# Ten x buffers, and a new order of openings, row copies and weight decode at the start of a convolution-gate kernel

## The chip, the cores and the metric

The kernel runs on one core of a Trainium2 chip. A core has five engines that run side by side, each taking its own instructions in order: TensorE (PE, matrix products; PEld in the profile is its weight load), VectorE (DVE), ScalarE (ACT), GpSimd (POOL) and SyncE (SP, which here only issues transfers). Sixteen DMA engines move data between the main memory and the core's memory SBUF, and inside SBUF. Matrix products are written to PSUM, which has eight banks. The metric is the time of one execution on the device in microseconds (us), smaller is better.

## What is computed

The input x has 8 sequences of 4224 positions with 192 channels. Two stages follow each other:

```python
# stage 1: a causal 7-tap convolution, taps by softmax, one set for each of 8 heads of 24 channels
w = exp(weight - weight.max(-1)); w = w / (w.sum(-1) + 1e-9)
x = einsum('hk,bskhg->bshg', w, windows_of_7(x))
# stage 2: a gated projection
gate = sigmoid(sum_k conv_w[k] * x[s - 4 + k])       # causal, 5 taps, each channel by itself
out = (gate * (x @ w_val)) @ w_out                   # two 192 x 192 products
```

All of it is float32.

## The kernel before

**Layout.** The sequences are joined into two long streams of 4 sequences each, which are computed side by side. 192 channels don't fit on 128 partitions, so 128 channels of both streams stand in a tile `x1` (two parts of columns), and the other 64 channels of both streams stand in `x2` (64 partitions for each stream).

**Superblocks and blocks.** The streams are cut into 13 superblocks (`NJS` has their sizes: 2, 3, ten times 5, 2), and each superblock into blocks of at most 502 columns: 2 blocks for each of superblocks 0 and 1, 3 for superblocks 2 to 11, one for the last. That makes 35 blocks. Block 0 and 1 have 304 and 302 columns, 2 and 3 have 448, the others 502, the last 364.

**Convolution (stage 1).** For each superblock the input comes as tiles `x_i` (`load_x`, line 131): four for superblock 0, then eight for each, one head apiece; they live in a pool of `XBUFS` buffers. `conv_unit` (line 271) computes a unit: four products of a window of x with a band matrix of the taps into one PSUM tile `pc` (line 285; each product stands as two instructions in the profile), and one copy on ACT from PSUM into `e` (line 294). Superblock 0 has 4 units, superblock 1 has 6, the others 10. As soon as a head is complete, `scatter` (line 306) issues the row copies: transfers from `e` to the rows of `x1` and `x2` (line 318, `x<-e` in the profile), on SP, or for heads 5 to 7 of the first three superblocks on POOL. Next to it `load_x` fetches the tile that takes the freed buffer.

**Gate and products (stage 2).** For each block n:
- `gate_open(n, i)` (line 343): ACT multiplies the x columns by the first of the five taps into a PSUM tile, `pa` (i = 0, both parts of `x1`) or `pb` (i = 1, `x2`). There is one `pa` and one `pb`. It needs the row copies of the block's superblock.
- `gate_taps` (line 354): DVE adds the other four taps (line 359).
- `gate_close` (line 364): ACT takes the sigmoid into `g1` or `g2` (line 372).
- `split` (line 458): ACT rounds x to its high part (lines 380, 388), POOL subtracts to get the low part (lines 381, 389), so that three fast products stand for one exact product.
- `diagonal`, `main`, `columns`, `rows` (lines 408 to 456): PE's products with `w_val` (what = "v") and `w_out` (what = "o"), into three PSUM tiles for each block and weight.
- `gated(n, q)` (line 464): DVE multiplies gate and value (line 468), which frees the PSUM tile of the value. `split_gated1` and `split_gated2` split the result.
- `project(n, q)` (line 478): ACT copies the output out of PSUM (line 484) and SP stores it.

The PSUM tiles of units, values and outputs share one pool of five buffers (`ps`, line 113).

**Weights.** They arrive as 64-bit floats, as pairs of integers. `decode` (line 203) makes float32 of them with nine DVE instructions (lines 212 to 222) on 128 x 384 elements and five more (line 228); `cast` (line 253) rounds the high part on ACT (line 255) and subtracts on DVE (line 256).

**Order.** The order of every engine's instructions is the order in which they are written; nothing is rearranged. The prologue (lines 514 to 532) decodes the small weights and `wv`, convolves superblocks 0 and 1, decodes `wo`, and opens the gates of blocks 0 and 1. Then step n of the main loop (line 534) works on the value of block n, the output of block n-1, the taps of block n+1, the opening of block n+2, and convolves `todo` units of the superblock that comes two after the one in work (`due`, line 505): 5 units in each of steps 0 to 3, then 3 or 4.

Of the kernel before, what the change touches and what calls it, by code (L numbers as in the profile page):

```python
# [81 lines left out]
PERM += [5 * HC + i for i in range(8, HC)]  # L82
QUADS = ((6, 7, 5, 0), (1, 2, 3, 4))
PER_LOAD = {2: 2, 3: 1, 5: 1}
XBUFS, EBUFS = 6, 3
LAG = 2
BY_POOL = 3

# [2 lines left out]
def kernel(  # L91
# [39 lines left out]
    def load_x(upto):  # L131
        while loaded[0] < min(upto, len(loads)):
            i = loaded[0]
            loaded[0] += 1
            g, hs, o = loads[i]
            f = len(hs) * NJS[g] * M
            t = xtiles[i] = xin.tile([WK, NMAX * M], F32, tag="x", name=f"x_{i}")
            nc.sync.dma_start(t[:, :f], xw[o : o + WK * f].rearrange("(p f) -> p f", f=f))
# [23 lines left out]
    def load_raw(name):  # L162
        nc.sync.dma_start(raw[name][1], raw[name][2])

    load_raw("cw")
    load_raw("wv")
    load_x(4)
    load_raw("wo")
    load_x(XBUFS)

    one = cp.tile([128, 1], F32, name="one")
# [86 lines left out]
    w_val, w_out = Weight("wv"), Weight("wo")  # L258
# [10 lines left out]
    first_unit = [next(i for i, u in enumerate(units) if u[0] == g) for g in range(NG)] + [len(units)]  # L269

    def conv_unit(u):
        g, q, ws = units[u]
        n = NJS[g]
        if u == first_unit[g]:
            x1s[g] = xp.tile([128, 2 * XB], F32, tag="x1", name=f"x1_{g}")
            x2s[g] = xp.tile([128, XC], F32, tag="x2", name=f"x2_{g}")
        if ws[0] == (0, 0):
            es[g, q] = ep.tile([M, 4 * NMAX * WIN], F32, tag="e", name=f"e_{g}_{q}")
        e = es[g, q]
        pc = ps.tile([128, 512], F32, tag="p", name=f"pc_{u}")  # L280
        for k, (hi, j) in enumerate(ws):
            h = QUADS[q][hi]
            i, at = home[g, h]
            c = (at * n + j) * M
            nc.tensor.matmul(  # L285
                pc[:M, k * WIN : (k + 1) * WIN],
                lhsT=xtiles[i][:, c : c + M],
                rhs=band[:, 4 * q + hi, :],
                start=True,
                stop=True,  # L290
            )
        a = (ws[0][0] * n + ws[0][1]) * WIN
        w = len(ws) * WIN
        nc.scalar.copy(e[:, a : a + w], pc[:M, :w])  # L294
        done = [hi for hi, j in ws if j == n - 1]
        for hi in done:
            h = QUADS[q][hi]
            i, at = home[g, h]
            last = at == len(loads[i][1]) - 1
            if last and g >= BY_POOL:  # L300
                load_x(i + 1 + XBUFS)
            scatter(g, h, e[:, hi * n * WIN : (hi + 1) * n * WIN])
            if last and g < BY_POOL:
                load_x(i + 1 + XBUFS)
# [28 lines left out]
    def views(n, k=KG - 1):  # L333
        g, o, m = STEPS[n]
        b = second(NJS[g])
        x1v = x1s[g][:, : 2 * b].rearrange("p (a t) -> p a t", a=2)
        return x1v[:, :, o + k : o + k + m], x2s[g][:, o + k : o + k + m]
# [5 lines left out]
    def gate_open(n, i):  # L343
        if n >= N:
            return
        m = STEPS[n][2]
        if i == 0:
            acc = ps_g.tile([128, 2, 512], F32, tag="pa", name=f"pa_{n}")[:, :, :m]
        else:
            acc = ps_h.tile([128, 512], F32, tag="pb", name=f"pb_{n}")[:, :m]  # L350
        accs[n, i] = acc
        nc.scalar.mul(acc, views(n, 0)[i], cwt[:, i, 0:1])  # L352

    def gate_taps(n, i, k0=1, k1=KG):
        if n >= N:
            return
        acc = accs[n, i]
        for k in range(k0, k1):
            nc.vector.scalar_tensor_tensor(  # L359
                out=acc, in0=views(n, k)[i], scalar=cwt[:, i, k : k + 1],  # L360
                in1=acc, op0=ALU.mult, op1=ALU.add,
            )

    def gate_close(n, i):
        if n >= N:
            return
        m = STEPS[n][2]
        if i == 0:
            dst = g1s[n] = gp.tile([128, 2, MB], F32, tag="g1", name=f"g1_{n}")[:, :, :m]
        else:  # L370
            dst = g2s[n] = gp.tile([128, MB], F32, tag="g2", name=f"g2_{n}")[:, :m]
        nc.scalar.activation(dst, accs.pop((n, i)), AF.Sigmoid)  # L372
# [35 lines left out]
    def diagonal(what, n):  # L408
        if not ok(n):
            return  # L410
        acc = bank(what, n, 2)
        w, _, _, h2, l2 = operands(what, n)
        r = slice(W22, W22 + 128)
        for i, (a, b) in enumerate(parts(w, h2, l2)):
            nc.tensor.matmul(acc, lhsT=a[:, r], rhs=b, start=(i == 0), stop=False)  # L415

    def main(what, n, q):
        if not ok(n):
            return
        fresh = (what, n, q) not in banks  # L420
        acc = bank(what, n, q) if fresh else banks[what, n, q]
        w, h, l, _, _ = operands(what, n)
        r = slice(W11, W11 + 128)
        for i, (a, b) in enumerate(parts(w, h, l)):
            nc.tensor.matmul(  # L425
                acc, lhsT=a[:, r], rhs=b[:, q], start=(fresh and i == 0), stop=(not fresh and i == 2)
            )
# [14 lines left out]
    def columns(what, n):  # L442
        if not ok(n):
            return
        m = STEPS[n][2]
        acc = banks[what, n, 2]
        w = w_val if what == "v" else w_out
        x = views(n)[0] if what == "v" else g1s[n]
        cuts = [m * i // 4 for i in range(5)]
        for i in range(4):  # L450
            c = slice(cuts[i], cuts[i + 1])
            for q, p in enumerate(HALVES):
                nc.tensor.matmul(  # L453
                    acc[p, c], lhsT=w.f[:, W12 : W12 + 64], rhs=x[:, q, c],
                    start=False, stop=(i == 3),
                )

    def split(n):
        if n >= N:
            return  # L460
        x1, x2 = views(n)
        xs[n, 1], xs[n, 2] = split1(sp, "x", n, x1), split2(sp, "x", n, x2)

    def gated(n, q):
        if not ok(n):
            return
        v = g1s[n][:, q] if q < 2 else g2s[n]
        nc.vector.tensor_tensor(out=v, in0=banks.pop(("v", n, q)), in1=v, op=ALU.mult)  # L468

    def split_gated1(n):  # L470
        if ok(n):
            pr[n, 1] = split1(pp, "p", n, g1s[n])

    def split_gated2(n):
        if ok(n):
            pr[n, 2] = split2(pp, "p", n, g2s[n])

    def project(n, q):
        if not ok(n):
            return  # L480
        m = STEPS[n][2]
        if n not in ots:
            ots[n] = op.tile([128, 3 * MB], F32, tag="ot", name=f"ot_{n}")
        nc.scalar.copy(ots[n][:, q * m : (q + 1) * m], banks.pop(("o", n, q)))  # L484
        o = 3 * sum(s[2] for s in STEPS[:n])
        if n == LAST:
            nc.sync.dma_start(out[:, o + q * m : o + (q + 1) * m], ots[n][:, q * m : (q + 1) * m])
        elif q == 1:
            nc.sync.dma_start(out[:, o : o + 3 * m], ots[n][:, : 3 * m])
# [3 lines left out]
    first = [next(n for n in range(N) if STEPS[n][0] == g) for g in range(NG)] + [N]  # L493
# [3 lines left out]
    done = [0]  # L497

    def conv(k):
        for _ in range(k):  # L500
            if done[0] < len(units):
                conv_unit(done[0])
                done[0] += 1
# [11 lines left out]
    put(cwt.rearrange("p a k -> p (a k)"), pr_cw, 0, 128, 0, 2 * KG)  # L515
    w_val.decode()
    conv(first_unit[1])
    w_val.cast()
    conv(2)
    w_out.decode()  # L520
    conv(1)
    gate_open(0, 0)
    gate_open(0, 1)
    gate_taps(0, 0)
    gate_taps(0, 1)
    split(0)
    w_out.cast()
    conv(first_unit[LAG] - done[0])
    gate_close(0, 0)
    gate_close(0, 1)  # L530
    gate_open(1, 0)
    gate_open(1, 1)

    for n in range(N + 1):
        todo = max(0, (due[n] if n < N else 0) - done[0])
        diagonal("v", n)
        gate_taps(n + 1, 0, 1, 3)
        split(n + 1)
        diagonal("o", n - 1)
        main("v", n, 0)  # L540
        main("v", n, 1)
        gate_taps(n + 1, 0, 3, KG)
        columns("v", n)
        gated(n, 2)
        gate_close(n + 1, 0)
        gate_open(n + 2, 0)
        columns("o", n - 1)
        split_gated2(n)
        project(n - 1, 2)
        rows("v", n)  # L550
        gated(n, 0)
        gated(n, 1)
        rows("o", n - 1)
        split_gated1(n)
        main("o", n - 1, 0)
        gate_taps(n + 1, 1)
        project(n - 1, 0)
        main("o", n - 1, 1)
        project(n - 1, 1)
        conv(todo)  # L560
        gate_close(n + 1, 1)
        gate_open(n + 2, 1)


# [88 lines left out]
```

## Time and profile before

| | us |
|---|---|
| median of 3 runs | 406.97 (405.59 to 406.98) |
| the profiled execution | 406.11 |
| its span in the profile | 404.3 |
| PE busy | 373.3 (92% of the span) |
| DVE busy | 347.1 (86%) |
| ACT busy | 320.3 (79%) |
| POOL busy | 249.7 (62%) |
| mean granted clock of PE | 0.974 of full speed |
| moved by DMA | 82.49 MB, 204 GB/s |

How to read the rows of the profile. A row of the order of instructions has the start and the length in us, the engine, the line of the kernel, the operation, the output and the inputs by their names, shapes, and how many instructions stand together (x4); in brackets stands the idle time of the engine just before it, and who ended it. A row of the chain of waits has start, length, engine, output and line; it follows the work that ended last back through what released it, so a row "DMA x<-e" is the time from the issue of a row copy until it landed. A row of the waits has the waiting engine, its tile and line, who released it, the total in us, how many times, and the longest. Both the tiles of the input and `x1`, `x2` are named x in the profile.

### The profile page before, as it was taken

To read this page: it belongs to the slowest core of one execution; us is meant where nothing else is said; L and a number is where in the kernel's file an instruction comes from. 1 tells how busy PE (TensorE), PEld (TensorE's weight loads), DVE (VectorE), ACT (ScalarE), POOL (GpSimd) and SP (SyncE) were. 2 spreads that over 40 slices of the span, in tenths; PEclk is the share of its full clock that TensorE was granted. 3 is DMA by queue.
4 is the path that set the end of the run, shared out by engine and by line. 5 is a ranking of instruction groups with operands and counts; after the bars stand their busy time and mean duration, and the time that the engine had idled before them with its cause. 6 is when DMAs were issued, how large, how long until landed. Compare 5 with 4: busy or idle time off the path is not lost.

```text
span 404.3 us, 8347 instructions
## 1 busy us (share of the span) xinstructions
PE 373.3 (92%) x3082; PEld 315.7 (78%) x3082; DVE 347.1 (86%) x435; ACT 320.3 (79%) x508; POOL 249.7 (62%) x170
## 2 busy tenths in 40 slices
PE   1685967999999999999999999999999999899896
PEld 1675966888888888888888888888888888676674
DVE  4888865689899899899999989989989989999971
ACT  4465937888888888888888988888888888788754
POOL 0834933666566666666666666666666656676772
PEclk9959996999999999999999999999999999999999
DMA  7697884886997897798698698698698696232233
GB/s 240 186 239 216 180 248 135 214 248 187 215 271 222 186 274 245 158 266 255 167 251 256 186 233 254 182 225 265 186 204 260 192 212 213 99 124 100 79 150 136
DMA packets 37884, 82.49 MB, mean 204 GB/s; under 512 B 5548, under 2 KB 16564, under 8 KB 37844
## 3 DMA queue, kind: packets, MB, share of 16 engines
q1 hardware_dynamic: 36756, 80.22, 70.0%
q0 software_dynamic: 1088, 1.74, 2.1%
q8 instruction: 24, 0.39, 0.5%
q14 instruction: 16, 0.13, 0.1%
HBM read 29.34 MB, written 26.00 MB: 137 GB/s over the span
## 4 chain that ended last, share of the span: by engine, by line
PE 85%; DMA 6%; DVE 4%; ACT 1%; issue 1%; SPq 1%; ACTq 0%; DVEq 0%
PE pc L285 22%; PE o L425 12%; PE v L425 11%; PE v L453 8%; PE o L453 7%; PE v L438 7%; PE o L438 6%; PE v L415 6%; PE o L415 6%; DMA x<-e 4%; DMA x<-xw 1%; DMA band<-bw 1%; DVE g L468 1%; DVE pa L359 1%; DVE pb L359 1%
## 5 line engine op out<-in xcount | busy, mean ns | idle before, releaser
L359 DVE SCALAR_TENSOR_TENSOR pa<-x,cwt,pa 128x1004 f32<-128x1004 f32 (+4 forms) x140 | 172.1, 1229 | 10.5 <-ACT pa L352 5.9
L285 PE MATMUL pc<-band,x 128*120 128x122 f32 x912 | 109.0, 279 | 20.8 <-DVE band L197 8.3
L285 PEld LDWEIGHTS pc<-band,x 128*120 128x120 f32 x912 | 107.1, 193 | 24.3 <-DVE band L197 8.3
L381 POOL TENSOR_TENSOR xl<-x,xh 128x1004 fp32r<-128x1004 f32 (+4 forms) x35 | 73.3, 2095 | 79.5 <-ACT xh L380 67.7
L359 DVE SCALAR_TENSOR_TENSOR pb<-x,cwt,pb 128x502 f32<-128x502 f32 (+4 forms) x140 | 101.3, 724 | 3.7
L468 DVE TENSOR_TENSOR g<-v,g 128x502 f32<-128x502 f32 (+4 forms) x105 | 65.6, 657 | 28.3 <-PE v L438 18.3
L381 POOL TENSOR_TENSOR pl<-g,ph 128x1004 fp32r<-128x1004 f32 (+4 forms) x35 | 79.0, 2256 | 7.8 <-ACT ph L380 6.7
L389 POOL TENSOR_TENSOR pl<-g,ph 128x502 fp32r<-128x502 f32 (+4 forms) x35 | 42.8, 1222 | 50.5 <-ACT ph L388 50.5
L372 ACT ACTIVATE g<-pa 128x1004 f32<-128x1004 f32 (+4 forms) x35 | 34.3, 980 | 46.2 <-DVE pa L359 20.6
L294 ACT COPY e<-pc 120x488 f32<-120x488 f32 x114 | 59.0, 587 | 6.7 <-PE pc L285 6.5
L484 ACT COPY ot<-o 128x502 f32<-128x502 f32 (+4 forms) x105 | 55.3, 561 | 1.6 <-PE o L425 0.9
L352 ACT ACTIVATE pa<-x,cwt 128x1004 f32<-128x1004 f32 (+4 forms) x35 | 37.5, 1072 | 14.8 <-DMA x<-e 9.6
L389 POOL TENSOR_TENSOR xl<-x,xh 128x502 fp32r<-128x502 f32 (+4 forms) x35 | 41.2, 1178 | 0.0
L453 PEld LDWEIGHTS v<-x,wvf 128*64 128x64 f32 x560 | 28.8, 136 | 12.0 <-issue 11.7
L453 PE MATMUL v<-x,wvf 128*64 128x125 f32 (+5 forms) x560 | 36.8, 272 | 0.0
L380 ACT CAST ph<-g 128x1004 fp32r<-128x1004 f32 (+4 forms) x35 | 34.9, 998 | 1.0 <-DVE g L468 1.0
L453 PE MATMUL o<-g,wof 128*64 128x125 f32 (+5 forms) x560 | 35.2, 266 | 0.0
L380 ACT CAST xh<-x 128x1004 fp32r<-128x1004 f32 (+4 forms) x35 | 34.4, 984 | 0.0
L453 PEld LDWEIGHTS o<-g,wof 128*64 128x64 f32 x560 | 30.6, 136 | 0.2 <-issue 0.2
L425 PE MATMUL o<-ph,woh 128*128 128x502 f32 (+4 forms) x70 | 30.4, 434 | 0.0
L425 PE MATMUL v<-xh,wvh 128*128 128x502 f32 (+4 forms) x70 | 27.4, 391 | 0.0
L425 PE MATMUL v<-xh,wvl 128*128 128x502 f32 (+4 forms) x70 | 27.3, 391 | 0.0
(74 smaller groups left out, 549.0 us busy)
## 6 DMA issues: line engine op xcount, KB each, us to landing
x<-xw SPq DMA_DIRECT2D x80, 300.0 KB
out<-ot SPq DMA_DIRECT2D x30, 753.0 KB
x<-e SPq DMA_DIRECT2D x50, 285.9 KB
x<-e SPq DMA_DIRECT2D x36, 141.6 KB
x<-xw SPq DMA_DIRECT2D x8, 240.0 KB
x<-e SPq DMA_DIRECT2D x18, 94.4 KB
x<-xw SPq DMA_DIRECT2D x8, 180.0 KB
out<-ot SPq DMA_DIRECT2D x2, 672.0 KB
```

What stands on the lines that cost most here:

```text
L285: nc.tensor.matmul(pc[:M, k * WIN : (k + 1) * WIN], lhsT=xtiles[i][:, c : c + M], rhs=band[:, 4 * q + hi, :], start=True, stop=True,)
L294: nc.scalar.copy(e[:, a : a + w], pc[:M, :w])
L359: nc.vector.scalar_tensor_tensor(out=acc, in0=views(n, k)[i], scalar=cwt[:, i, k : k + 1], in1=acc, op0=ALU.mult, op1=ALU.add,)
L380: nc.scalar.copy(h, x)
L381: nc.gpsimd.tensor_tensor(out=l, in0=x, in1=h.bitcast(F32), op=ALU.subtract)
L389: nc.gpsimd.tensor_tensor(out=l, in0=x, in1=h.bitcast(F32), op=ALU.subtract)
L415: nc.tensor.matmul(acc, lhsT=a[:, r], rhs=b, start=(i == 0), stop=False)
L425: nc.tensor.matmul(acc, lhsT=a[:, r], rhs=b[:, q], start=(fresh and i == 0), stop=(not fresh and i == 2))
L438: nc.tensor.matmul(acc, lhsT=a[p, r], rhs=b[p], start=(fresh and i == 0), stop=(not fresh and i == 2))
L453: nc.tensor.matmul(acc[p, c], lhsT=w.f[:, W12 : W12 + 64], rhs=x[:, q, c], start=False, stop=(i == 3),)
L468: nc.vector.tensor_tensor(out=v, in0=banks.pop(("v", n, q)), in1=v, op=ALU.mult)
L484: nc.scalar.copy(ots[n][:, q * m : (q + 1) * m], banks.pop(("o", n, q)))
```

## The change

Four things are changed, all of them about order and room; no arithmetic changes.

- The pool of x tiles has ten buffers instead of six. The loads at the start are x0, the small weights `cw`, x1, `wv`, and then x2 to x9. The load of `wo` is issued after superblock 0 has been convolved.
- The six units of superblock 1 are all convolved before the first gate is opened (three of them stood behind the first openings, taps and splits).
- In steps 0 to 3 (`early` is 4, the first block of superblock 2) `gate_open(n + 2, 0)` moves from behind the first closing to the end of the step, behind the convolution. In these steps the convolution is cut in two: `todo // 2` units ahead of `gate_close(n + 1, 1)`, the others behind it.
- `w_out.decode()` and `w_out.cast()` move from the prologue into step 0: the decode behind the last taps of that step, the cast behind its first two units.

```diff
-XBUFS, EBUFS = 6, 3
+XBUFS, EBUFS = 10, 3
...
     load_raw("cw")
+    load_x(2)
     load_raw("wv")
-    load_x(4)
-    load_raw("wo")
     load_x(XBUFS)
...
     conv(first_unit[1])
+    load_raw("wo")
     w_val.cast()
-    conv(2)
-    w_out.decode()
-    conv(1)
+    conv(first_unit[LAG] - done[0])
     gate_open(0, 0)
     gate_open(0, 1)
     gate_taps(0, 0)
     gate_taps(0, 1)
     split(0)
-    w_out.cast()
-    conv(first_unit[LAG] - done[0])
     gate_close(0, 0)
     gate_close(0, 1)
     gate_open(1, 0)
     gate_open(1, 1)
+
+    early = first[LAG]
...
         gate_close(n + 1, 0)
-        gate_open(n + 2, 0)
+        if n >= early:
+            gate_open(n + 2, 0)
...
         project(n - 1, 1)
-        conv(todo)
+        if n == 0:
+            w_out.decode()
+        part = todo if n >= early else todo // 2
+        conv(part)
+        if n == 0:
+            w_out.cast()
         gate_close(n + 1, 1)
+        conv(todo - part)
+        if n < early:
+            gate_open(n + 2, 0)
         gate_open(n + 2, 1)
```

## The prediction

> **What bounds the kernel now.** I read the table of stretches first, then the order of instructions on ACT, on DVE and on PE.
>
> ```profile
> span 404.3 us, 8347 instructions
> ```
> ```profile
> 39.00:43.00 4.00, 3.93 (x30) 3.65 (x32) 3.29 (x3) 3.97 (x9) 4.00 (x6) 0.59 0.27 70
> ...
> 63.00:69.00 6.00, 5.41 (x25) 5.38 (x26) 4.85 (x4) 4.10 (x10) 3.22 (x2) 0.50 0.49 159
> ...
> 79.00:320.00 241.00, 241.00 (x2022) 203.36 (x2021) 220.96 (x250) 209.37 (x326) 155.85 (x91) 1.00 0.82 228
> ```
>
> The columns are the stretch, its length, busy time of PE, PEld, DVE, ACT and POOL, the granted clock of PE, the DMA share and GB/s. From 79 to 320 us PE is busy all the time at full clock. Nothing the change does there can help, and a delay brought to 79 us is carried to the end. So the question is when PE reaches that stretch. Before it, three openings of gates (L352, on ACT) wait for row copies:
>
> ```profile
> 22.09 0.77 ACT L352 ACTIVATE pa<-x,cwt 128x608 f32<-128x608 f32 x1 [4.22 <-DMA x<-xw]
> ...
> 36.58 1.01 ACT L352 ACTIVATE pa<-x,cwt 128x896 f32<-128x896 f32 x1 [2.62 <-DMA x<-e]
> ...
> 61.64 1.10 ACT L352 ACTIVATE pa<-x,cwt 128x1004 f32<-128x1004 f32 x1 [6.96 <-DMA x<-e]
> ```
>
> They open blocks 0, 2 and 4, the first ones of superblocks 0, 1 and 2. While ACT stands there, the copies `e<-pc` behind it stand too, and with them PE. But DVE also has a chain:
>
> ```profile
> 16.85 0.35 DVE L212 TENSOR_SCALAR scr<-scr 128x384 int32<-128x384 int32 x1
> ...
> 21.06 0.99 DVE L228 TENSOR_TENSOR wof<-scr,scr 128x128 f32<-128x128 f32 x5
> 22.89 3.53 DVE L359 SCALAR_TENSOR_TENSOR pa<-x,cwt,pa 128x608 f32<-128x608 f32 x4 [0.84 <-DMA x<-xw]
> ...
> 28.62 0.56 DVE L256 TENSOR_TENSOR wol<-wof,woh 128x384 fp32r<-128x384 f32 x1
> ...
> 34.31 2.24 DVE L359 SCALAR_TENSOR_TENSOR pb<-x,cwt,pb 128x302 f32<-128x302 f32 x4
> 37.63 4.73 DVE L359 SCALAR_TENSOR_TENSOR pa<-x,cwt,pa 128x896 f32<-128x896 f32 x4 [1.07 <-ACT pa L352]
> 43.24 0.47 DVE L468 TENSOR_TENSOR g<-v,g 128x302 f32<-128x302 f32 x1 [0.88 <-ACT xh L388]
> 44.30 0.85 DVE L468 TENSOR_TENSOR g<-v,g 128x302 f32<-128x302 f32 x2 [0.59 <-PE v L438]
> 45.07 2.86 DVE L359 SCALAR_TENSOR_TENSOR pb<-x,cwt,pb 128x448 f32<-128x448 f32 x4
> 47.83 4.72 DVE L359 SCALAR_TENSOR_TENSOR pa<-x,cwt,pa 128x896 f32<-128x896 f32 x4
> 53.28 0.63 DVE L468 TENSOR_TENSOR g<-v,g 128x448 f32<-128x448 f32 x1 [0.72 <-PE v L453]
> ...
> 62.78 5.18 DVE L359 SCALAR_TENSOR_TENSOR pa<-x,cwt,pa 128x1004 f32<-128x1004 f32 x4 [4.27 <-ACT pa L352]
> ...
> 78.35 5.17 DVE L359 SCALAR_TENSOR_TENSOR pa<-x,cwt,pa 128x1004 f32<-128x1004 f32 x4
> 84.24 0.68 DVE L468 TENSOR_TENSOR g<-v,g 128x502 f32<-128x502 f32 x1 [0.72 <-PE v L453]
> ```
>
> The decode of `wo` (16.85 to 22.05, 5.20 us) lies in a hole: DVE's next work starts at 22.89, when the first gate is open. From there to 36.55 DVE has taps and products of blocks 0 and 1 almost without a pause. And the taps of block 3 (47.83) run while PE convolves, because their gate was opened in the middle of step 1.
>
> **The change, part by part.**
>
> *Ten buffers, new load order, second superblock first.* Before the first gate PE waits for loads:
>
> ```profile
> PE pc L285 <- DMA x<-xw: 5.1, 3, 2.6
> ```
>
> With x6 to x9 fetched early this goes, and the second superblock's six units pass PE ahead of the first gate. What is late next is the first gate, which opens at 22.09 when the first superblock's row copies are in. Their issue hangs on the same units and copies as before. Three more `e` copies (0.57 each, 1.7) now go ahead of that opening, inside its wait of 4.22. Behind it DVE's chain sets the pace. I take 0. Bounds: the opening comes at best 4.22 - 1.7 = 2.5 us sooner; at worst its last copy, issued at 17.12 and in before 22.09, takes as long as the slowest landing on the chain, 7.50, and is 2.5 us later.
>
> ```profile
> 17.12 0.77 SPq L318
> ...
> 29.52 6.83 DMA x<-e
> ...
> 40.20 0.76 PE o L415 x3
> ...
> 44.27 0.42 PE o L438 x6
> 44.69 1.05 PE o L425 x6
> 45.74 4.20 PE pc L285 x40
> ...
> 54.04 7.50 DMA x<-e
> ...
> 74.19 0.60 PE o L438 x6
> 74.79 1.43 PE o L425 x6
> ...
> 80.42 0.69 PE v L415 x3
> ...
> 85.75 0.62 PE o L438 x6
> ```
>
> Deeper prefetch also puts four more loads ahead of the second superblock's last row copy, in by 36.35 (29.52 + 6.83). At 300 KB each and the 228 GB/s above that is 1.35 us apiece, 5.4 in all: in by 41.8 at worst. The sum needs them at 44.2, so this costs 0.
>
> *`wo` decoded behind the first products.* On DVE it now follows the last taps of step 0, which end at 36.55, so it runs from 36.55 to 41.75. The hole at 16.85 stays empty. Behind it on ACT stands the cast of `wo`, and behind the cast the closing of block 1's second gate, three `e` copies and the opening of block 2:
>
> ```profile
> 24.17 0.51 ACT L255 CAST woh<-wof 128x384 fp32r<-128x384 f32 x1
> ...
> 40.75 0.46 ACT L372 ACTIVATE g<-pb 128x302 f32<-128x302 f32 x1
> ...
> 49.98 0.57 ACT L294 COPY e<-pc 120x488 f32<-120x488 f32 x1 [0.28 <-PE pc L285]
> ...
> 64.88 1.52 ACT L294 COPY e<-pc 120x488 f32<-120x488 f32 x3
> ```
>
> 41.75 + 0.51 + 0.46 + 1.52 + 1.01 = 45.25: the taps of block 2 start there instead of 37.63, **7.6 us later**. The wait of 2.62 for the copies is gone, but the decode and its cast have taken its place. Who waits behind that cast: PE, for the PSUM banks that the three copies free and for the cast weights; DVE, for block 2's opening; SP and POOL, whose row copies of those units come later. POOL's low parts of block 2 stand behind those, but PE needs them only after step 1's convolutions, over 10 us on. The load of `wo` itself goes on SP behind the loads up to x13, all issued by some 19 us; with the slowest landing, 7.50, it is in by 27 and needed at 36.55: 0.
>
> *Gates open behind the row copies (steps 0 to 3).* The opening of block n+2 now stands behind all of step n's convolutions. So tap chain and convolution, which overlapped, follow each other: taps of n+1, product of n (it frees the PSUM bank that PE's rows of `o` need), rows and main of `o`, 40 convolution matmuls, the last `e` copy, the opening.
> - Step 1: 4.73 + 0.47 + 0.42 + 1.05 + 4.20 + 0.57 + 1.01 = 12.45
> - Step 2: 4.72 + 0.63 + 1.47 + 4.20 + 0.57 + 1.10 = 12.69
> - Step 3: 5.18 + 0.63 + 0.60 + 1.43 + 4.20 + 0.57 + 1.10 = 13.71
>
> Together 38.85, against 40.72 now (78.35 - 37.63), of which the wait of 6.96 is a part: the removed wait is worth 1.9 us net. The third superblock's row copies are issued before block 3's opening ends (57.7) and in by some 65 (57.7 + 7.50), ahead of the opening at 69, so that wait does go.
>
> Block 5's taps start at 45.25 + 38.85 = 84.1 instead of 78.35. Block 4's product ends at 84.1 + 5.17 + 0.68 = 89.95; today PE is at the rows of `o` of that step at 85.75. PE is **4.2 us late** there, at the mouth of the stretch where it is never idle. DVE's later chains need less than PE's steps (220.96 busy of 241), so it adds nothing more and recovers nothing.
>
> *Clock.* The new chains leave PE idle in each step. In step 1 PE starts at 42.8 (41.75 + 0.51, and 0.56 for the low part on DVE), works 44.27 - 40.20 = 4.1 us, then waits for the product at 50.45: a gap of 3.5 us. Steps 2 and 3: the copy, opening, taps and product take 6.9 and 7.5, PE's own work in it 4.1 to 5.3 (85.75 - 80.42): gaps of 1.6 to 3.4. Gaps of the trace:
>
> ```profile
> 33.69 2.78 PE L285 MATMUL pc<-band,x 128*120 128x122 f32 x24 [1.52 <-DVE g L468]
> ```
> ```profile
> 39.07 0.62 PE L415 MATMUL v<-xh,wvh 128*128 128x302 f32 x1 [2.61 <-ACT e L294]
> ```
> ```profile
> 63.59 5.23 PE pc L285 x24
> ```
>
> After 1.52 us idle the clock held (24 matmuls in 2.78, against 5.23 at half clock); after 2.61 the granted clock was 0.59 (39 to 43), after some 6 us 0.50 (63 to 69). The loss is busy time by the missing clock: 3.93 x 0.41 = 1.6 and 5.41 x 0.50 = 2.7. Step 1's gap is past 2.61, so it is cold: I take 2.0, between the two. Steps 2 and 3 lie across the border: 0 taken, up to 2.7 each as bound.
>
> [...]
>
> **Sum:** +7.6 - 1.9 = 5.7 at block 5's taps, of which PE feels 4.2; with the clock +6.2. The profiled execution took 406.11, 1.8 around its span, the median of the runs is 406.97; I start from 406.5, between them: **412.7 us**. About 0.5% (2 us) is what a measurement of this kernel tells from no change.
>
> **Rivals.**
> 1. *Faster.* The early steps aren't chained through the convolutions. Place: the opening of block 3. If PE convolves and copies step 1's units beside the taps, that step needs only DVE's own work, 4.73 + 0.47 + 0.85 + 2.86 = 8.91, which is 3.5 less; three steps 10.6: 406.5 + 4.2 - 10.6 = 400.1. It decides from that opening's end: 54.2 instead of 57.7. For it: the waits of 2.62 and 6.96 are real, and units are ready early. Against it: PE's rows of `o` come ahead of the convolutions in its queue and need a bank that only the product frees. It also covers a decode that finds room I don't see. 0.18.
> 2. *Slower still.* The clock falls in steps 2 and 3 as well, 2.0 each: 416.7; with 2.7 three times 418.8. Against it: the gaps are at the border. 0.15.
> 3. *No change.* The first gate opens 2.5 us sooner and the clock holds: 406.5 + 4.2 - 2.5 = 408.2. For it: 4.22 us of wait is left to shrink. Against it: nothing in the diff makes those copies issue sooner. 0.12.
>
> That ten buffers change nothing by themselves is part of the forecast, not a rival.
>
> **How the numbers follow.** The forecast has 0.55, its own range is 410 to 415 (clock 0 to 2.7 in step 1, and some landing). Slower holds 0.55 + 0.15 = 0.70, same 0.12, faster 0.18. The range reaches up to 419 over the second rival and down to 402, into the first, so that under 0.2 is left out.
>
> **What would show it.** In the changed profile: DVE's `scr` group right behind the taps near 36.5, with an empty stretch before 22.9; ACT's `woh` cast waiting for it; the opening of block 2 ending near 45 with no wait for DMA; taps of blocks 3, 4, 5 starting 12 to 15 us apart, each just behind an opening; half clock around 50; block 4's product near 90. The prediction is wrong if block 2 is opened before 41, if the taps of block 3 start before 55, or if PE idles somewhere after 90 us where it doesn't now.

## The result, and the profile after

The changed kernel is slower, twice as much as forecast. Of its four runs, 417.48, 418.31, 422.58 and 1250.02 us, the last was disturbed and is left out, as such runs are below. That leaves a median of 418.31 us, against 406.33 us for the kernel before (4 runs); the ratio of the means is 1.0324, with an interval of 1.0235 to 1.0412. The profiled execution took 418.31 us, its span is 416.5 (before: 406.11 and 404.3): 12.2 us more where 6.2 were forecast.

The line numbers of the functions are one smaller in the changed kernel: the opening is L351, the taps L358, the product L467, the convolution L284, its copy L293. In the kernels of the experiments they shift by one or a few. First the order of instructions on DVE, after:

```profile
24.68 3.53 DVE L358 SCALAR_TENSOR_TENSOR pa<-x,cwt,pa 128x608 f32<-128x608 f32 x4 [7.79 <-DMA scr<-wo]
...
42.71 0.99 DVE L227 TENSOR_TENSOR wof<-scr,scr 128x128 f32<-128x128 f32 x5
46.97 4.73 DVE L358 SCALAR_TENSOR_TENSOR pa<-x,cwt,pa 128x896 f32<-128x896 f32 x4 [2.07 <-ACT pa L351]
...
59.59 4.73 DVE L358 SCALAR_TENSOR_TENSOR pa<-x,cwt,pa 128x896 f32<-128x896 f32 x4 [3.99 <-ACT pa L351]
...
75.49 5.18 DVE L358 SCALAR_TENSOR_TENSOR pa<-x,cwt,pa 128x1004 f32<-128x1004 f32 x4 [6.81 <-DMA x<-xw]
...
90.91 5.18 DVE L358 SCALAR_TENSOR_TENSOR pa<-x,cwt,pa 128x1004 f32<-128x1004 f32 x4 [5.66 <-ACT pa L351]
```

The taps of blocks 0, 2, 3, 4 and 5 start at 24.68, 46.97, 59.59, 75.49 and 90.91. The decode, from 38.26 to 43.70, stands behind the taps of blocks 0 and 1, as forecast, and the hole ahead of 24.68 is empty. Two releasers in brackets must not be taken at their word: the row at 24.68 names the load of `wo` and the row at 75.49 an x tile, but taps use neither. ACT's order of instructions tells what they waited for:

```profile
22.48 1.50 ACT L293 COPY e<-pc 120x488 f32<-120x488 f32 x3 [4.77 <-DMA x<-e]
23.86 0.80 ACT L351 ACTIVATE pa<-x,cwt 128x608 f32<-128x608 f32 x1
...
43.79 0.51 ACT L254 CAST woh<-wof 128x384 fp32r<-128x384 f32 x1 [5.94 <-DVE wof L227]
...
44.52 1.49 ACT L293 COPY e<-pc 120x488 f32<-120x488 f32 x3
45.89 1.05 ACT L351 ACTIVATE pa<-x,cwt 128x896 f32<-128x896 f32 x1
...
74.35 1.11 ACT L351 ACTIVATE pa<-x,cwt 128x1004 f32<-128x1004 f32 x1
```

The openings end at 24.66, 46.94 and 75.46, just ahead of the taps. Ahead of the first one stand three copies to `e`. There are three `e` buffers, and these copies wait until row copies of superblock 0 have left one of them. Ahead of the opening of block 2 stands the cast of `wo`, for which ACT stood idle 5.94 us, until the decode was done.

Now PE, in its order of instructions: the waits, and in the table of stretches the granted clock behind them (columns: stretch, length, busy time and instructions of PE, clock, DMA share, GB/s).

```profile
44.36 0.62 PE L414 MATMUL o<-ph,woh 128*128 128x304 f32 x1 [5.67 <-ACT woh L254]
...
52.12 0.40 PE L437 MATMUL o<-ph,woh 64*128 64x304 f32 x1 [1.27 <-DVE g L467]
...
64.90 0.62 PE L437 MATMUL o<-ph,woh 64*128 64x302 f32 x1 [2.21 <-DVE g L467]
...
81.25 0.47 PE L437 MATMUL o<-ph,woh 64*128 64x448 f32 x1 [2.24 <-DVE g L467]
...
96.73 0.47 PE L437 MATMUL o<-ph,woh 64*128 64x448 f32 x1 [1.94 <-DVE g L467]
```
```profile
40.74:50.98 10.24, 6.50 (x48) 0.50 0.50 124
64.64:71.47 6.83, 6.57 (x30) 0.50 0.67 185
...
81.70:85.12 3.42, 3.42 (x14) 0.50 0.18 62
361.60:365.00 3.40, 3.40 (x11) 0.50 0.00 0
```

Before, PE was at the rows of `o` of that last step at 85.75; now at 96.73, so 10.98 us of the 12.2 are there when the long full stretch begins. The other 1.2 come near the end, where 3.4 us ran at half clock (before: clock 1.00 from 362 to 366). Behind the waits of 2.21 and 2.24 us the clock is at half, and that is on the path. The chain of waits shows it as longer work (start, length, engine, output, line):

```profile
82.36 2.54 PE o L424 x6
```

The six products (L424; L425 before) that took 1.43 us before (74.79) take 2.54.

The shift, place by place, against the prediction's sum:

| | predicted | measured |
|---|---|---|
| first taps (22.89 before) | 0 | 24.68: +1.8 |
| decode and cast, up to block 2's taps | +7.6 | 46.97 - 37.63 - 1.8: +7.5 |
| the three steps 1 to 3 (40.72 before) | 38.85: -1.9 | 90.91 - 46.97 = 43.94: +3.2 |
| sum at block 5's taps | +5.7 | +12.6 |
| felt by PE at its rows of `o` | +4.2 | +11.0 |
| clock beside that | +2.0 | +1.2, near the end |
| end | +6.2 | +12.2 |

So two theories had to be told apart. **A:** the late decode costs 6 to 7.5 us, and the half clock in steps 2 and 3 some 5 more; the late openings by themselves would be about even. **B:** the late openings chain the steps through the convolutions, and it is that, or a wait for transfers that the ten buffers bring, which costs the 5 us, whatever the clock.

### The profile page after: what moved, and what is told of

The parts are those of the page before. It is cut to its first block, busy times and chain, and to the rows that moved or that the text cites. A ratio compares the mean times of both kernels' runs of the same rounds, so it can differ in the third digit from the quotient of the medians.

```text
span 416.5 us, 8353 instructions
## 1 busy us (share of the span) xinstructions
PE 378.7 (91%) x3082; PEld 319.2 (77%) x3082; DVE 346.8 (83%) x435; ACT 320.9 (77%) x508; POOL 250.1 (60%) x170
## 4 chain that ended last, share of the span: by engine, by line
PE 78%; DVE 10%; DMA 5%; issue 3%; ACT 2%; POOL 1%; SPq 0%; DVEq 0%; ACTq 0%
PE pc L284 20%; PE o L424 13%; PE v L424 9%; PE v L452 7%; PE o L452 6%; PE o L437 6%; PE v L437 6%; DVE pa L358 5%; PE o L414 5%; PE v L414 5%; DMA x<-e 3%; DVE g L467 2%; DVE pb L358 1%; DMA band<-bw 1%; ACT pa L351 1%
## 5 line engine op out<-in xcount | busy, mean ns | idle before, releaser
L358 DVE SCALAR_TENSOR_TENSOR pa<-x,cwt,pa 128x1004 f32<-128x1004 f32 (+4 forms) x140 | 172.1, 1229 | 31.2 <-ACT pa L351 12.9
L284 PEld LDWEIGHTS pc<-band,x 128*120 128x120 f32 x912 | 106.7, 193 | 11.5 <-DVE band L196 8.2
L284 PE MATMUL pc<-band,x 128*120 128x122 f32 x912 | 107.2, 277 | 8.6 <-DVE band L196 8.2
L358 DVE SCALAR_TENSOR_TENSOR pb<-x,cwt,pb 128x502 f32<-128x502 f32 (+4 forms) x140 | 101.3, 724 | 3.7
L467 DVE TENSOR_TENSOR g<-v,g 128x502 f32<-128x502 f32 (+4 forms) x105 | 65.2, 655 | 19.5 <-PE v L437 16.5
L293 ACT COPY e<-pc 120x488 f32<-120x488 f32 x114 | 59.6, 585 | 14.2 <-PE pc L284 9.2
L452 PEld LDWEIGHTS v<-x,wvf 128*64 128x64 f32 x560 | 29.7, 141 | 12.0 <-issue 12.0
L351 ACT ACTIVATE pa<-x,cwt 128x1004 f32<-128x1004 f32 (+4 forms) x35 | 37.6, 1074 | 0.9
L452 PE MATMUL v<-x,wvf 128*64 128x125 f32 (+5 forms) x560 | 37.9, 279 | 0.0
L424 PE MATMUL o<-ph,woh 128*128 128x502 f32 (+4 forms) x70 | 31.6, 452 | 0.0
L437 PE MATMUL o<-ph,woh 64*128 64x502 f32 (+4 forms) x70 | 18.2, 408 | 12.0 <-DVE g L467 12.0
L424 PE MATMUL o<-pl,woh 128*128 128x502 f32 (+4 forms) x70 | 28.0, 400 | 0.0
```

The source lines that it names most:

```text
L284: nc.tensor.matmul(pc[:M, k * WIN : (k + 1) * WIN], lhsT=xtiles[i][:, c : c + M], rhs=band[:, 4 * q + hi, :], start=True, stop=True,)
L358: nc.vector.scalar_tensor_tensor(out=acc, in0=views(n, k)[i], scalar=cwt[:, i, k : k + 1], in1=acc, op0=ALU.mult, op1=ALU.add,)
L424: nc.tensor.matmul(acc, lhsT=a[:, r], rhs=b[:, q], start=(fresh and i == 0), stop=(not fresh and i == 2))
L437: nc.tensor.matmul(acc, lhsT=a[p, r], rhs=b[p], start=(fresh and i == 0), stop=(not fresh and i == 2))
L452: nc.tensor.matmul(acc[p, c], lhsT=w.f[:, W12 : W12 + 64], rhs=x[:, q, c], start=False, stop=(i == 3),)
```

## The experiments

Times are medians; each ratio is one of means, to runs of the kernel before on the same chip (medians 405.8 to 406.1 us), with its interval. Names with a_ start from the changed kernel, b_ from the kernel before; c_ are combinations. The start of a run varies: PE's first product came at 7.30 to 8.94 us in the profiles (8.27 before, 8.23 in the changed kernel). So places in two traces can differ by about 1 us for that alone.

### The decode, taken back and put in alone

a_decode_early is the changed kernel with the load, decode and cast of `wo` where they were; b_decode_late is the kernel before with only the decode and cast moved into step 0 (and the convolution of that step cut in two around the cast).

```diff
# a_decode_early
     load_raw("wv")
+    load_x(4)
+    load_raw("wo")
     load_x(XBUFS)
...
-    load_raw("wo")
     w_val.cast()
     conv(first_unit[LAG] - done[0])
+    w_out.decode()
...
     split(0)
+    w_out.cast()
...
-        if n == 0:
-            w_out.decode()
...
-        if n == 0:
-            w_out.cast()
```

> The changed kernel with the load, the decode and the cast of wo back at their old places (the decode now behind the six units, the cast behind the split of block 0). Theory of the cast: block 2's taps start at 46.97 in the changed kernel because decode and cast (38.26 to 44.30) stand ahead of that opening; without them ACT needs only the row copies (in at 39.2) and three copies of 1.49, so they start near 41 and the whole is 5 to 6 us shorter, about 412 to 414. Theory of the openings: all of the loss is in the chained steps and the clock; it stays within 2 us of the changed kernel's 418. Theory of the loads: the same, and block 2's opening waits for a row copy past 44.

> The kernel before with only the decode and the cast of wo moved into step 0 (the convolution of that step cut in two around the cast, the load where it was). Theory of the cast: decode from 36.5 to 41.8, block 2's taps start near 43 instead of 37.6, and of these 5 us some 3 to 5 are left at the end: 409 to 412. Theory of the openings: the delay disappears in the wait for the row copies of superblock 2 (7 us at 54 to 61), within 2 us of before.

a_decode_early took 411.74 us, 1.0143 (1.0108 to 1.0179). b_decode_late took 409.6 us, 1.0089 (1.0072 to 1.0106). Both are near what the theory of the cast expected. DVE's order in a_decode_early:

```profile
40.47 4.73 DVE L360 SCALAR_TENSOR_TENSOR pa<-x,cwt,pa 128x896 f32<-128x896 f32 x4 [2.80 <-ACT pa L353]
...
54.63 4.73 DVE L360 SCALAR_TENSOR_TENSOR pa<-x,cwt,pa 128x896 f32<-128x896 f32 x4 [5.52 <-ACT pa L353]
...
67.50 5.18 DVE L360 SCALAR_TENSOR_TENSOR pa<-x,cwt,pa 128x1004 f32<-128x1004 f32 x4 [3.79 <-ACT pa L353]
...
84.42 5.18 DVE L360 SCALAR_TENSOR_TENSOR pa<-x,cwt,pa 128x1004 f32<-128x1004 f32 x4 [7.15 <-ACT pa L353]
```

Block 2's taps start 6.5 us sooner than in the changed kernel (40.47 for 46.97), and block 5's by the same. The opening of block 2 starts at 39.38, so no row copy holds it past 44, and the theory of the loads falls. In b_decode_late block 2's taps go from 37.63 to 43.49, just behind the cast (rows of ACT and of DVE):

```profile
42.47 0.51 ACT L255 CAST woh<-wof 128x384 fp32r<-128x384 f32 x1 [3.05 <-DVE wof L228]
```
```profile
43.49 4.72 DVE L359 SCALAR_TENSOR_TENSOR pa<-x,cwt,pa 128x896 f32<-128x896 f32 x4
```

Its first taps start 1.0 us sooner than before (21.91 for 22.89), so behind them the delay is 6.8 us, of which 3.5 are left at the end. The decode's cost at block 2's taps is thus shown from both sides. What the steps do is left: 14.16, 12.87 and 16.92 us in a_decode_early, and the long ones (the first and the third) are those in which the clock was at half (45.70 to 49.11 and 73.01 to 79.83).

### What moves the first opening and the row copies

Three kernels: b_ten_bufs has only the ten buffers, b_conv_ahead only the six units of superblock 1 ahead of the first gate, and a_ebufs4 is the changed kernel with a fourth `e` buffer (one run).

```diff
# b_ten_bufs
-XBUFS, EBUFS = 6, 3
+XBUFS, EBUFS = 10, 3
# a_ebufs4
-XBUFS, EBUFS = 10, 3
+XBUFS, EBUFS = 10, 4
# b_conv_ahead
-    conv(2)
+    conv(first_unit[LAG] - done[0])
     w_out.decode()
-    conv(1)
...
-    conv(first_unit[LAG] - done[0])
     gate_close(0, 0)
```

> The kernel before with ten x buffers and nothing else. My forecast said 0 for this: within 2 us of before, 404.5 to 408.5, with block 2's opening at 36.6 to 41. Theory of the loads: four more loads ahead of the row copies make the openings of blocks 2 and 4 wait longer, 3 to 5 us each, and the whole is 3 us or more longer.

> The kernel before with only one part of the change: all six units of superblock 1 convolved ahead of the first gate (six x buffers, openings and wo's decode and cast at the old places but for the order). Theory of the e buffers: the three copies to e of the second half wait for the row copies of superblock 0, the first opening goes from 22.1 to 23 to 24 and the first taps to 24 to 25, and about 1.5 us of it stays to block 5's taps (79.5 to 81): 407-409, ratio 1.002-1.007. As predicted (nothing): first taps within 0.5 of 22.9 and 405.5-406.8, ratio 0.998-1.001. Gain theory: the units leave TensorE's queue behind the first gate, and block 2's opening comes before 36.6: below 405.5.

> The changed kernel with four e buffers instead of three. Theory: in the changed kernel the copies of superblock 1's second half wait 4.77 us for row copies of superblock 0 that read the same buffer, and the first opening (23.86) stands behind these three copies; with a buffer of their own they are done near 19.5, and the first opening starts at 22.4 to 22.7, as soon as the last row copy is in. The whole is 1 to 1.5 us shorter. Otherwise the opening stays at 23.9.

b_ten_bufs took 407.41 us, 1.0032 (1.0012 to 1.0053). ACT's order of instructions:

```profile
39.12 1.01 ACT L352 ACTIVATE pa<-x,cwt 128x896 f32<-128x896 f32 x1 [5.26 <-DMA x<-xw]
...
64.35 1.10 ACT L352 ACTIVATE pa<-x,cwt 128x1004 f32<-128x1004 f32 x1 [7.27 <-DMA x<-e]
```

The opening of block 2 comes 2.5 us later than before (36.58), that of block 4 2.7 us later. Only the depth of the loads differs, so it is the loads that delay the row copies; that they stand ahead of them in the queue is argued, since the trace doesn't give each landing, and the bracket at 39.12 names an x tile, which an opening doesn't read. This is the delay that the prediction bounded at 5.4 us, and it costs about 1.3 us as soon as nothing else delays that opening.

b_conv_ahead took 407.78 us, 1.0051 (1.0027 to 1.0074). The size is near what the theory of the `e` buffers expected, but its mechanism was missed: with six x buffers PE waits for loads as before (four waits, 5.5 us in all; before three, 5.1 us), and the first opening now stands behind the copies of the units that these loads feed. The last of those copies starts at 26.88, and the first taps start at 28.15, not near 24.5. The ten buffers are needed for this part, and each of the two alone costs time.

a_ebufs4 took 418.95 us in its one run, no gain. All copies to `e` are done by 20.7, and it is the row copies again that release the first opening. In ACT's order:

```profile
22.95 0.77 ACT L351 ACTIVATE pa<-x,cwt 128x608 f32<-128x608 f32 x1 [2.25 <-DMA x<-e]
```

The opening starts 0.9 us sooner than in the changed kernel, although PE's first product was some 0.7 us later in this run (8.94 for 8.23). So the wait for an `e` buffer is what the first opening lost; the time didn't follow (1 to 1.5 us less were expected), and one run with its own stretches of half clock leaves the worth at the end unsettled.

### The openings, taken back and put in alone

a_gates_mid is the changed kernel with the four openings at their old place (`early = 0`). b_defer4 is the kernel before with only the four openings moved; b_defer2 moves only those of blocks 2 and 4, the ones that waited for row copies.

```diff
# b_defer4; b_defer2 has late = (0, 2) for the test n < early
-        gate_open(n + 2, 0)
+        if n >= early:
+            gate_open(n + 2, 0)
...
-        conv(todo)
+        part = todo if n >= early else todo // 2
+        conv(part)
         gate_close(n + 1, 1)
+        conv(todo - part)
+        if n < early:
+            gate_open(n + 2, 0)
```

> The changed kernel with every opening back behind the first closing; all else as changed. Theory of the openings: the three chained steps (12.6, 15.9, 15.4 us from taps to taps) get back to 10 to 13 us, but openings wait for row copies again (near 39 for block 2, past 60 for block 4); block 2's taps start near 45, and the whole gets 4 to 8 us shorter, 410 to 414. Theory of the cast: it hardly moves, under 2 us, since the decode stays where it is.

> The kernel before with only the four openings put behind the convolutions of their steps (convolution cut in two as in the change); six buffers, old loads, decode where it was. Theory of the chain: block 2's opening no longer waits, but stands behind three copies: taps near 39; then three chained steps of 12.6 to 15.9 us; block 5's taps at 78 to 84 against 78.35, the whole 406 to 412. Theory that the openings pay by themselves and only the decode harms: the waits of 2.6 and 7.0 us are won, 398 to 403.

> The kernel before with only the openings of blocks 2 and 4 put behind the convolutions (steps 0 and 2): these are the two that wait for new row copies; blocks 3 and 5 need none and open in the middle of their steps as before. Theory of the chain: taps of block 2 near 39, of block 3 near 49 (step 1 overlaps as before, about 10 us), of block 4 at 62 to 65, of block 5 at 73 to 77 against 78.35, the whole 401 to 405, faster than before by up to 1%. If the removed waits only move to another place, it stays at 406.

a_gates_mid took 411.78 us, 1.0145 (1.0108 to 1.0182); b_defer4 408.72 us, 1.0078 (1.0048 to 1.0108); b_defer2 405.03 us, 0.9985 (0.9963 to 1.0007), just past the upper end of what the theory expected and not to be told from no change. In a_gates_mid the waits for transfers are back, as in the kernel before: the openings of blocks 2 and 4 start at 39.30 and 67.73 after waits of 4.89 and 6.94 us, and block 5's taps start at 83.44, where the changed kernel has 90.91. Block 2's taps still start behind the decode, at 45.01. The whole is 6.5 us shorter than the changed kernel, as the theory of the openings expected (410 to 414). But this kernel can't tell A from B: it takes away the chain and, with it, PE's waits of some 2 us for the products.

In b_defer4 the steps follow each other through the convolutions; DVE's order:

```profile
38.43 4.73 DVE L359 SCALAR_TENSOR_TENSOR pa<-x,cwt,pa 128x896 f32<-128x896 f32 x4 [2.79 <-ACT pa L352]
...
53.55 4.73 DVE L359 SCALAR_TENSOR_TENSOR pa<-x,cwt,pa 128x896 f32<-128x896 f32 x4 [6.48 <-ACT pa L352]
...
67.95 5.18 DVE L359 SCALAR_TENSOR_TENSOR pa<-x,cwt,pa 128x1004 f32<-128x1004 f32 x4 [5.32 <-ACT pa L352]
...
81.87 5.18 DVE L359 SCALAR_TENSOR_TENSOR pa<-x,cwt,pa 128x1004 f32<-128x1004 f32 x4 [4.16 <-ACT pa L352]
```

15.12, 14.40 and 13.92 us a step; again the two at half clock are over the sums for full clock (12.45 and 12.69), and the one at full clock is on it (13.71). In b_defer2 blocks 3 and 5 are opened in the middle of their steps, so their taps run beside the convolution as before:

```profile
63.88 5.18 DVE L359 SCALAR_TENSOR_TENSOR pa<-x,cwt,pa 128x1004 f32<-128x1004 f32 x4 [3.96 <-ACT pa L352]
...
73.56 5.17 DVE L359 SCALAR_TENSOR_TENSOR pa<-x,cwt,pa 128x1004 f32<-128x1004 f32 x4
82.62 0.68 DVE L468 TENSOR_TENSOR g<-v,g 128x502 f32<-128x502 f32 x1 [3.89 <-PE v L453]
```

Block 5's taps start 4.8 us sooner than before (73.56 for 78.35), but the next product only 1.6 (82.62 for 84.24): DVE stands 3.89 us there for PE's value. Of both, 1.3 us are an earlier start (first taps at 21.55 for 22.89), so hardly anything of the gain reaches the product. PE's waits and clock say why:

```profile
43.17 0.62 PE L438 MATMUL o<-ph,woh 64*128 64x304 f32 x1 [3.86 <-DVE g L468]
...
69.65 0.74 PE L438 MATMUL o<-ph,woh 64*128 64x448 f32 x1 [2.95 <-DVE g L468]
```
```profile
41.31:48.14 6.83, 4.97 (x23) 0.50 0.57 121
68.62:75.45 6.83, 5.80 (x21) 0.50 0.57 150
```

### The clock, held by idle products

If it is the clock, filling PE's waits must give the time back without changing any order. a_keep_warm is the changed kernel with products into the first PSUM tile of `o`, ahead of the real ones that overwrite them; 15 for block 1 and 10 for blocks 2 and 3. (The first rows of `o` wait only for the second tile, so the idle products fit into the wait.)

```diff
# a_keep_warm, in rows(what, n)
-        two = [bank(what, n, q) if fresh else banks[what, n, q] for q in range(2)]
         w, _, _, h2, l2 = operands(what, n)
+        two = [bank(what, n, 0) if fresh else banks[what, n, 0]]
+        if fresh and n in (1, 2, 3):
+            for _ in range(15 if n == 1 else 10):
+                nc.tensor.matmul(two[0], lhsT=w.h[:, W22:W22 + 128], rhs=h2, start=True, stop=True)
+        two.append(bank(what, n, 1) if fresh else banks[what, n, 1])
```

> The changed kernel with 15, 10 and 10 added matmuls in steps 2, 3 and 4, into the PSUM tile of the output whose real products begin afresh behind them; they lie in the gap in which PE waits for the product of the step (2.2, 2.2 and 1.9 us in the changed kernel) and nothing waits for them. Theory of the clock: those gaps let the clock fall to half in steps 2 and 3; filled, the steps last 12.6 to 13.7 us from taps to taps instead of 15.9 and 15.4, and the whole is 3 to 6 us shorter than the changed kernel, 412 to 415. Theory of the chain alone: the steps keep their lengths, and the whole stays at 417 to 420.

It took 413.41 us, 1.0201 (1.016 to 1.0243), some 5 us less than the changed kernel's 418.31. DVE's order, and PE's clock in the stretches that were at half in the changed kernel:

```profile
46.72 4.73 DVE L358 SCALAR_TENSOR_TENSOR pa<-x,cwt,pa 128x896 f32<-128x896 f32 x4 [2.07 <-ACT pa L351]
...
60.88 4.73 DVE L358 SCALAR_TENSOR_TENSOR pa<-x,cwt,pa 128x896 f32<-128x896 f32 x4 [5.53 <-ACT pa L351]
...
73.76 5.18 DVE L358 SCALAR_TENSOR_TENSOR pa<-x,cwt,pa 128x1004 f32<-128x1004 f32 x4 [3.79 <-ACT pa L351]
...
87.65 5.18 DVE L358 SCALAR_TENSOR_TENSOR pa<-x,cwt,pa 128x1004 f32<-128x1004 f32 x4 [4.12 <-ACT pa L351]
```
```profile
64.64:71.47 6.83, 6.83 (x59) 1.00 0.85 233
81.70:85.12 3.42, 3.42 (x35) 1.00 0.67 242
```

Steps 2 and 3 now take 12.88 and 13.89 us, where the changed kernel took 15.90 and 15.42 and the prediction's sums for a full clock were 12.69 and 13.71. Theory B falls for these 5 us: the order is the same, and 4.55 us are gone. Step 1, whose wait for block 0's product (2.14 us, up to 51.88) had no idle products, became longer, 14.16 for 12.62, with the clock at half from 51.94 to 55.35. From there on it was full until 410 us.

### Both costs taken away

c_early_warm is a_decode_early with 24, 14, 9 and 8 idle products for blocks 0 to 3. Ten buffers, the convolutions ahead and the four late openings remain.

```diff
# on a_decode_early, with the code of a_keep_warm
+            for _ in range({0: 24, 1: 14, 2: 9, 3: 8}.get(n, 0)):
```

> The changed kernel with two of its suspected costs taken away at once: wo's load, decode and cast at the old places, and 24, 14, 9 and 8 idle matmuls of TensorE in the waits for the products of blocks 0 to 3 (3.87, 2.20, 2.25 and 1.94 us where only the decode was moved). What is left of the change are ten buffers, the second superblock ahead of the first gate and the four late openings. If the decode and the clock carry the loss, the three steps take about 12.5, 12.7 and 13.7 us as the prediction's sums for a full clock, block 5's taps start at 40.5 + 38.9 = 79.4 (84.42 where only the decode was moved), no half clock is seen after 45, and the time is 406-409, ratio 1.000-1.007. Rival: the row copies, or another wait that the half clock hid, hold the steps; then they stay at 14 us or more with a full clock and the time is 410 or more.

It took 406.51 us, 1.0013 (0.9993 to 1.0033). DVE's order:

```profile
40.97 4.73 DVE L360 SCALAR_TENSOR_TENSOR pa<-x,cwt,pa 128x896 f32<-128x896 f32 x4 [2.79 <-ACT pa L353]
...
53.61 4.73 DVE L360 SCALAR_TENSOR_TENSOR pa<-x,cwt,pa 128x896 f32<-128x896 f32 x4 [4.00 <-ACT pa L353]
...
66.50 5.18 DVE L360 SCALAR_TENSOR_TENSOR pa<-x,cwt,pa 128x1004 f32<-128x1004 f32 x4 [3.79 <-ACT pa L353]
...
80.39 5.18 DVE L360 SCALAR_TENSOR_TENSOR pa<-x,cwt,pa 128x1004 f32<-128x1004 f32 x4 [4.13 <-ACT pa L353]
```

The steps are 12.64, 12.89 and 13.89 us, each within 0.2 of the sums, and the granted clock is 1.00 from 45 to 100 us:

```profile
45.00:100.00 55.00, 54.84 (x454) 1.00 0.75 204
```

So without the late decode and with the clock held, nothing of the 3.2% loss is left that these runs can tell. That doesn't make the rest of the change free: the kernel before has its own stretch at half clock (63 to 69), which c_early_warm has not, and c_defer2_warm below, also held at full clock but without most of this rest, is 1.3% faster than c_early_warm.

### A version faster than both

c_defer2_warm is b_defer2 with 24 idle products for block 0 and 12 for block 2, the two waits shown above; c_defer2_warm_tail has 3 and 5 more for the two waits of 0.88 and 1.42 us near the end.

```diff
# on b_defer2, with the code of a_keep_warm
+            for _ in range({0: 24, 2: 12}.get(n, 0)):
```

> The kernel before with only the openings of blocks 2 and 4 moved behind the convolutions, and with 24 and 12 idle matmuls of TensorE (into the first o bank, overwritten by the real product) in the two waits that the same kernel showed without them: 3.86 us ahead of block 0's rows of o (43.17) and 2.95 us ahead of block 2's (69.65). Clock theory: the openings' gain of 4.8 us at block 5's taps (73.56 instead of 78.35) was lost because TensorE ran at half clock at 41.3-48.1 and 68.6-75.5; with the waits filled neither stretch is there, block 4's product ends its wait near 79-80 instead of 82.62, and the time is 400-403, ratio 0.985-0.993. Rival: the matmuls' order, not the clock, holds block 4's product; then it stays at 82 to 83 with a full clock, and the time is 404.5-406.5, ratio 0.997-1.001. Third: idle matmuls delay the real ones by their own length; then both gaps are gone and the rows of o come later than 43.2 and 69.7.

> As c_defer2_warm, with 3 and 5 more idle matmuls in the waits of 0.88 and 1.42 us near the end (the rows of o at 368 and 378). If the half clock of one stretch of 3.4 us near the end (379.2-382.7 in the kernel without idle matmuls) comes from those waits, it is gone in every run and the time is 0.5 to 1.5 us below c_defer2_warm; if such a stretch is a matter of where the clock's steps of 3.4 us happen to fall in one run, the two have the same time within 0.5 us.

c_defer2_warm took 400.88 us, 0.9878 (0.9857 to 0.9899): 1.2% faster than the kernel before, as the clock theory expected. The clock in the same two stretches as in b_defer2, and the product of block 4 in DVE's order:

```profile
41.31:48.14 6.83, 6.72 (x55) 1.00 0.55 107
68.62:75.45 6.83, 6.83 (x56) 1.00 0.71 183
```
```profile
78.53 0.68 DVE L472 TENSOR_TENSOR g<-v,g 128x502 f32<-128x502 f32 x1 [1.27 <-PE v L457]
```

The product comes at 78.53 instead of 82.62, 5.7 us ahead of the kernel before (84.24), and the span is 5.6 us shorter (398.7). About 1.0 us of both is an earlier start (first taps at 21.88 for 22.89); the medians differ by 5.1 us. The kernel before with idle products alone was not run, so how the gain divides between the two openings and the clock is open. The third expectation fell: the idle products run inside the waits, and the rows of `o` go on at 42.98 and 68.17, not later than without them (43.17 and 69.65).

c_defer2_warm_tail took 402.41 us, 0.9901 (0.9873 to 0.993). Its interval overlaps the other's, and its median is 1.5 us longer, which neither of the two expectations foresaw. It has no half clock from 360 to 384, but neither has the profile of c_defer2_warm, so filling the late waits brought nothing.

## Why the prediction was wrong

The direction was right, and so was the largest term; the time, 412.7 with a range up to 419, was too low: 6.2 us were forecast and 12.2 measured.

- **Decode and cast: right.** +7.6 forecast, +7.5 in the trace, and the mechanism is shown by a_decode_early and b_decode_late (6.5 and 6.8 us): the cast of `wo` stands on ACT ahead of the copies and the opening of block 2.
- **First opening: missed by 1.8 us.** The prediction let three more copies to `e` run "inside its wait of 4.22". They can't: there are three `e` buffers, and the copies wait for row copies of superblock 0, as the opening does. They then stand ahead of it with 1.50 us. The bound of +2.5 held, for another reason than the one given.
- **Ten buffers: right for this kernel, wrong as a statement on its own.** The opening that needs the row copies does come 2.5 us later (b_ten_bufs). In the changed kernel the late decode covers that; without the cover it costs 1.3 us.
- **Three chained steps: the sums were right, the clock in them wrong.** This is the step that failed: "Steps 2 and 3 lie across the border: 0 taken". With the clock held the runs gave 12.64, 12.89 and 13.89 us for 12.45, 12.69 and 13.71. In the changed kernel steps 2 and 3 cost 3.2 and 1.7 us over the sums, together 4.9: the first is past the bound of 2.7, and both are far from the 0 taken. The gaps were forecast as 1.6 to 3.4 us, measured 2.21 and 2.24.
- **Clock in step 1: 2.0 taken, about 0.2 measured.** PE was at half clock from 40.74 to 50.98, about where it was forecast, but behind another wait: the clock fell while PE stood 5.67 us for the cast (up to 44.36). The gap for the product, forecast as 3.5 us, was 1.27 us (up to 52.12), since PE's work ahead of it took 6.5 us at half clock where 4.1 were reckoned. That slow work lay beside the taps of block 2 (46.97 to 51.60), which set the end of that stretch. The loss, busy time by missing clock, counted here only where PE was what the next step waited for: 0.2 us over the sum in step 1, 3.2 and 1.7 us in steps 2 and 3. In steps 2 and 3 the slow products and the convolution stand between a product of DVE and the next opening, with nothing beside them.
- **Slack of PE: right.** 12.56 us at block 5's taps became 10.98 at the rows of `o`, as 5.7 became 4.2 in the sum: 1.6 us are swallowed there, 1.5 in the sum.
- **After 90 us:** PE idles 1.94 us once more at 96.73, which the prediction named as a sign against it, and 3.4 us near the end ran at half clock. Together with the stretch behind it the tail cost 1.2 us.

So the second rival, "the clock falls in steps 2 and 3 as well", was what happened; it was given 0.15. With its 2.0 for each of those steps and with the first opening's 1.8, the sum would have been 412.7 + 4.0 + 1.8 = 418.5, near the measured 418.31; that it is so near is partly chance, since the 2.0 of step 1 stands in it for a cost that came elsewhere. The point from which it decides was in reach: the trace of before held the clock after 1.52 us and lost it at 2.61, and the forecast gaps, 1.6 to 3.4 us, reach past that. The first rival, faster by chains that don't pass the convolutions, failed where it was said to decide: the opening of block 3 ended at 59.56, near the 57.7 of the sum with the first opening's 1.8, not at 54.2.

What stays open: how much the wait for `e` buffers costs at the end (a_ebufs4 was one run), and what decides whether 3.4 us near the end run at half clock: they did in the profiles of the changed kernel, of b_ten_bufs (382.6 to 386.0) and of b_defer2 (379.2 to 382.7, behind a wait of 1.42 us), not in that of the kernel before, which has a wait of 1.41 us there.

## What to carry to other kernels

Moving a wait behind an engine's other work is worth what it frees only if the things that follow don't then stand in a chain: here two openings that had really waited for transfers brought their taps forward (the whole gained only with TensorE's waits filled, in c_defer2_warm), and two that hadn't lost the overlap of taps and convolution. A step that is moved onto an in-order queue is charged with all that stands behind it there; the decode of 5 us cost 7.5 through one cast. And where a change makes TensorE wait some 2 us at a time, the clock is part of the price (half clock came here with waits of 1.94, 2.21 and 2.24 us, though not with every wait of that length): look whether slow work lies on the path, and if so fill the waits.

## What the hardware showed that was not expected

**Waits of the same length, two outcomes.** In b_defer4 PE waited 2.21 us up to 58.85 and 2.25 us up to 73.71, and behind the first the clock was at half for 3.41 us, behind the second not:

```profile
59.26:62.67 3.41, 3.41 (x17) 0.50 0.64 172
73.71:77.12 3.41, 3.41 (x23) 1.00 0.46 142
```

The stretches at half clock are 3.42, 6.83 and 10.24 us long in the changed kernel, that is one, two and three times 3.41. Waits of 2.21 and 2.24 us (up to 64.90 and 81.25) came with half clock there. In a_decode_early even one of 1.94 us did, where the changed kernel has a wait of the same 1.94 us (up to 96.73) without a fall:

```profile
90.24 0.74 PE L439 MATMUL o<-ph,woh 64*128 64x448 f32 x1 [1.94 <-DVE g L469]
```
```profile
90.07:96.90 6.83, 6.66 (x25) 0.50 0.34 124
```

In b_defer4 the first wait ends 0.41 us ahead of its stretch at half clock (58.85 for 59.26); in a_decode_early 1.77 of the 1.94 us lie ahead of the start of its stretch (90.07). What decides between the two outcomes, these runs don't show.

**Idle products cost nothing in a wait that held them.** In c_defer2_warm 24 of them took 3.63 us, and the rows of `o` behind them went on at 42.98, where they had gone on at 43.17 without them.
